# Attention, soft mixture and gated layer on one core: the gated layer issued step by step in an order from a list scheduler

## The chip, the cores and the metric

The kernel runs on one core of a Trainium2 chip. Its time is the device time of one execution in microseconds (us); the kernel before took 598.79 us, the median of three runs (597.3 to 600.0). A core has five engines that each work through an instruction queue of their own in order: TensorE (PE in the profile, its weight loads PEld), VectorE (DVE), ScalarE (ACT), GpSimd (POOL) and SyncE (SP), which here issues every DMA. They wait for each other through semaphores. Matrix products land in PSUM, the accumulator memory, which has eight banks; all else lives in SBUF.

## The reference

Three layers follow each other. Inputs are drawn in float32 (the gated layer's weights come to the kernel as 64-bit words).

```python
# 1: causal attention, 4 batches x 12 heads, 448 positions, head size 64
attn = softmax(mask(q @ k.T / 8)); x = attn @ v          # -> x: 1792 tokens x 768
# 2: soft mixture of 8 experts with 4 slots each
logits = x @ phi                                         # 1792 x 32
slot_input = softmax(logits, over tokens).T @ x          # 32 x 768
slot_out[e] = relu(slot_input[e] @ w1[e]) @ w2[e]        # w1 768x1024, w2 1024x768
x = softmax(logits, over slots) @ slot_out               # 1792 x 768, of rank 32
# 3: gated layer, 1536 hidden columns
out = (sigmoid(x @ w_gate) * (x @ w_val)) @ w_out        # 1792 x 768
```

Since x of layer 3 is (coefficients 1792x32) @ (slots 32x768), the kernel first forms slots @ w_gate and slots @ w_val (32 rows), and then multiplies by the coefficients.

## The kernel before

The attention and the mixture (the first 346 us of the trace) are not touched by the change. What follows is the gated layer.

The 1536 hidden columns are cut into six units u of 256 columns. A unit needs three weight pieces of 1.5 MB, named o, v and g (of w_out, w_val and w_gate), which SP loads in that order, two units ahead where a buffer is free: five buffers `w`. Each piece arrives as 64-bit floats and is turned into 32-bit floats in place by two ACT instructions (L193, L143) and two DVE instructions (L197, L199) over 1536 columns. Then:

- o: ACT finds the largest absolute value (L666), a matmul with ones spreads it over the partitions (`amx`, L138), DVE makes a power of two of it, and the piece is split into two float16 halves `wh` (L145 or L143) and `wl` (L674).
- v and g: twelve matmuls with the slots (`psg`, L685), a maximum on DVE (L688), a copy on ACT (`gh`, L689), a fold matmul (L693), and two float16 halves `st` (L702 on ACT, L704 on DVE).

The main work of a unit has two kinds of steps. A gate step takes one batch of 448 tokens and 128 hidden columns: two matmuls (`psg` L822 and `psv` L823), a sigmoid on ACT (`sg`, L828), the product on DVE (`hs`, L829), a float16 high part (`hhi`, L830, on ACT, DVE or POOL) and a low part on POOL (`hlo`, L831). There are eight gate steps in a unit. An output step takes one tile of 128 tokens: twelve matmuls of 384 columns (L849; 24 of half the rows where a tile lies across two batches, two tiles of 14) into two PSUM banks, `o0` and `o1`, two buffers each. Each half is then evicted and added to the accumulator `oacc` in SBUF: either DVE alone (L861), or ACT into `ev` (L143) and then POOL adds (L859). The first unit only writes `oacc`, without adding. After the last unit a tile is stored.

The order: the loops of the source say for each tile how many preparation steps of the next unit go beside it (`PPI`), and gate steps are issued `LA` = 4 tiles ahead; the framework's own scheduler then moves instructions by its estimates of time, so that the order on an engine is not that of the source. Only the weight loads are pinned to the order of the source (`PINW`). `HIE`, `EV`, `MWE` and `WHE` say by unit which engine makes `hhi`, the two evictions, the maximum and `wh`. The units' weight conversions are done early: by the time the first unit's tiles are out, the pieces of units 1 and 2 and part of unit 3's are converted.

`hid[b, u]` holds `hhi` and `hlo` of a batch and unit, in `NH` = 4 buffers.

Of the kernel before, what the change touches and what calls it, by code (L numbers as in the profile page):

```python
# [1 line left out]

# [5 lines left out]
F32 = mybir.dt.float32  # L8
# [11 lines left out]
def kernel(  # L20
# [44 lines left out]
    PARTS = ((0,), (1,), (2,), (3,), (4,), (5,))  # L65
# [7 lines left out]
    PPI = (1, 3, 3, 6, 4)  # L73
    LAG = 1
    LA = 4
    NH = 4
# [12 lines left out]
    PINW = True  # L89
    PB = (3, 3, 2)  # L90
    HIE = 'PPVAAAVAAAVV'
    EV = 'AAPVVPVVVPVV'
    MWE = 'AAAAAA'
    WHE = 'VVAAAV'
# [27 lines left out]

    def pow2(pool, mx, n, nm):
# [3 lines left out]
        nc.vector.tensor_scalar(p, mx, 2.0 ** -20, None, ALU.max)  # L127
        nc.vector.tensor_scalar(p.bitcast(I32), p.bitcast(I32), 0x7F800000, None, ALU.bitwise_and)
        nc.vector.reciprocal(s, p)
        nc.vector.tensor_scalar(s, s, P14, None, ALU.mult)  # L130
        return p, s

    def spread_sum(pool, ps_pool, tag, am):

        am16 = pool.tile([128, 1], BF16, tag="am16", name="am16")
        nc.vector.tensor_copy(am16, am)
        out_ = ps_pool.tile([128, 1], F32, tag=tag, name="amx")
        nc.tensor.matmul(out_, lhsT=ones, rhs=am16, start=True, stop=True)  # L138
        return out_

    def mult(on, out, in_, x):
        if on == "A":
            nc.scalar.activation(out=out, in_=in_, func=AF.Copy, scale=x)  # L143
        else:
            nc.vector.tensor_scalar(out, in_, x, None, ALU.mult)  # L145

# [18 lines left out]
    for u in range(len(PARTS[0]), FF // UC):  # L165
        worder += w_unit(u)

    wt = {}
    ring = [wpC] * NC + [wpA] * NA
    solo = []  # L170

    def load_w(n=1):
        for _ in range(n):
# [6 lines left out]
            x = nc.sync.dma_start(out=t.bitcast(I32) if key[0] in "ovg" else t, in_=src)  # L180
            if PINW:
                tc.keep_in_program_order(x)
            wt[key] = t

    def from_f64(key):

        t = wt[key].bitcast(I32).rearrange("p a (b w) -> p a b w", w=2)
        lo, hi = t[:, :, :, 0], t[:, :, :, 1]  # L190
        top = wt[key].bitcast(U16).rearrange("p a (b w) -> p a b w", w=4)[:, :, :, 1]

        nc.scalar.activation(out=lo, in_=top, func=AF.Copy, scale=2.0 ** -13, bias=2.0 ** -15 - 0.5)  # L193
        yield
        mult("A", hi.bitcast(F32), hi.bitcast(F32), 2.0 ** -112)
        yield
        nc.vector.scalar_tensor_tensor(lo, hi, -2 ** 31, lo, ALU.bitwise_and, ALU.bitwise_or)  # L197
        yield
        nc.vector.scalar_tensor_tensor(hi, hi, 3, lo, ALU.logical_shift_left, ALU.bitwise_or)  # L199
        yield  # L200
        return hi.bitcast(F32)


    with ExitStack() as actx:
# [28 lines left out]

        class Pinned:

            def __init__(self, engine):
                self.engine = engine

            def __getattr__(self, name):
                f = getattr(self.engine, name)  # L240

                def call(*a, **kw):
                    x = f(*a, **kw)  # L243
                    tc.keep_in_program_order(x)
                    return x
                return call
# [398 lines left out]
    gs_p = ctx.enter_context(rp("gs", 1))  # L645
    wo_p = {}
    st_p = {u: st0 for u in PARTS[0]}
# [6 lines left out]
    unit = [{} for _ in range(FF // UC)]  # L654
# [4 lines left out]
    def prep_o(u, wo):  # L659

        d = unit[u]
        mw = sm1("mw")
        wh = wo_p[u].tile([128, 2, DM], F16, tag=f"wh{(u - 1) % 4}", name="wh")
        wl = wo_p[u].tile([128, 2, DM], F16, tag=f"wl{(u - 1) % 4}", name="wl")
        if MWE[u] == "A":
            nc.scalar.activation(out=wl, in_=wo, func=AF.Abs, accum_out=mw)  # L666
        else:
            nc.vector.tensor_reduce(mw, wo, axis=AX.XY, op=ALU.max, apply_absolute_value=True)
        yield
        am = spread_sum(sm2, ps1, "a", mw)  # L670
        d["pw"], sw = pow2(sm2, am, 1, f"w{u}")
        mult(WHE[u], wh, wo, sw)
        yield
        nc.vector.scalar_tensor_tensor(wl, wo, sw, wh, ALU.mult, ALU.subtract)  # L674
        d["w"] = (wh, wl)
        yield

    def prep_gv(u, nm, w):

        d = unit[u]  # L680
        tg = "a" if nm == "g" else "b"
        ps = ps1.tile([128, UC], F32, tag=tg, name="psg")
        for kc in range(KC):
            g = kc % 4
            nc.tensor.matmul(ps[32 * g:32 * g + 32, :], lhsT=soT[:, kc], rhs=w[:, kc], start=kc < 4, stop=kc + 4 >= KC)  # L685
        gh = gs_p.tile([128, UC], F32, tag="gh", name="gh")
        mv = sm1("m" + nm)
        nc.vector.tensor_reduce(mv, ps, axis=AX.X, op=ALU.max, apply_absolute_value=True)  # L688
        nc.scalar.copy(gh, ps)  # L689
        yield  # L690
        ps = ps1.tile([128, UC], F32, tag=tg, name="psg2")
        mx = spread_sum(sm2, ps1, tg, mv)
        nc.tensor.matmul(ps, lhsT=fold4.rearrange("p a s -> p (a s)"), rhs=gh, start=True, stop=True)  # L693
        p, sc = pow2(sm2, mx, 1, f"{nm}{u}")
        if nm == "g":
            d["ag"] = sm1(f"ag{u}")
            nc.vector.tensor_scalar(d["ag"], p, 2.0 ** -28, None, ALU.mult)
        else:
            d["pv"] = p
        yield  # L700
        st = d[nm] = st_p[u].tile([128, UC], F16, tag=f"{nm}{(u - 1) % 4}", name="st")
        nc.scalar.activation(out=st, in_=ps, func=AF.Copy, scale=sc)  # L702
        yield
        nc.vector.scalar_tensor_tensor(st[64:], ps[64:], sc[64:], st[64:], ALU.mult, ALU.subtract)  # L704
        yield

    def prep(us):

        post = iter(())
        got = {}  # L710

        def conv(key):
# [225 lines left out]
```

## Time and profile before

| | us |
|---|---|
| median of 3 runs | 598.79 |
| the profiled execution | 598.05 |
| its span, first to last instruction | 596.2 |
| first output matmul of the gated layer | 355.13 |
| last output matmul starts | 591.62 |
| TensorE busy, share of the span | 508.3, 85% |
| VectorE / ScalarE / GpSimd busy | 389.8 / 326.6 / 248.6 |
| mean granted clock of TensorE | 0.956 |

The clock is given as a share of full speed: 1.00 is 2.4 GHz and 0.50 is 1.2 GHz, the two levels that occur. A matmul's duration includes its way through the array, and matmuls overlap: what one costs on a busy PE is the distance between the starts of two that follow each other. Instructions of DVE and ACT overlap by some tenths of a microsecond in the same way. A wait is idle time of an engine just before an instruction, put down to the instruction whose semaphore came last.

### The profile page before, as it was taken

The numbers are of one execution on the slowest core, as the hardware profiler recorded it, in microseconds if no ns is written. First come the engines' busy times: TensorE is split into PE (matmuls) and PEld (weight loads), VectorE is DVE, ScalarE is ACT, GpSimd is POOL, SyncE is SP. The second block draws the span as 40 slices with busy tenths as digits, with TensorE's granted clock in tenths as the row PEclk, the third lists the DMA queues.
The fourth block names the chain that finished last, engine by engine and source line by source line (L and its number), as shares of the span: only waits on it lengthen the run. The fifth ranks groups of instructions, "written<-read, shape, count | busy, mean of one in ns | idle before, by whom it ended". The sixth has DMA issues, their size and how long they took to land.

```text
span 596.2 us, 12985 instructions
## 1 busy us (share of the span) xinstructions
PE 508.3 (85%) x4977; PEld 308.1 (52%) x4977; DVE 389.8 (65%) x962; ACT 326.6 (55%) x734; POOL 248.6 (42%) x341
## 2 busy tenths in 40 slices
PE   2899989998999799799924678769989889899997
PEld 1576766675667576455412234434544435455554
DVE  2788877796877887321035038987975957774674
ACT  2677867676777667101152059997857753434400
POOL 6665663655466410000000028406775861445720
PEclk9899999999999999879978689998999989899999
DMA  7756547554674213879999991805305303000044
GB/s 161 199 116 183 159 144 200 160 136 125 182 199 127 80 28 108 317 291 382 404 399 404 407 396 70 300 18 197 121 1 212 107 1 107 0 1 1 2 186 185
DMA packets 95565, 101.59 MB, mean 170 GB/s; under 512 B 68624, under 2 KB 68624, under 8 KB 95504
## 3 DMA queue, kind: packets, MB, share of 16 engines
q1 hardware_dynamic: 95504, 100.77, 51.1%
q8 instruction: 39, 0.64, 0.5%
q14 instruction: 22, 0.18, 0.1%
HBM read 95.26 MB, written 5.51 MB: 169 GB/s over the span
## 4 chain that ended last, share of the span: by engine, by line
PE 60%; ACT 13%; DMA 10%; DVE 6%; issue 4%; POOL 4%; ACTq 0%; DVEq 0%; POOLq 0%; SPq 0%
PE pso L849 20%; PE psP L243 9%; PE psS L243 8%; ACT P L243 4%; DMA w<-in_moe_w_val_dram 4%; PE psX L243 4%; DMA w<-in_moe_w_dram 4%; PE psT L243 4%; PE psh L741 3%; PE so L754 3%; ACT hi L243 3%; DMA w<-in_moe_w_gate_dram 2%; PE psg L685 2%; ACT w L143 2%; DVE hs L829 1%
## 5 line engine op out<-in xcount | busy, mean ns | idle before, releaser
L849 PE MATMUL pso<-wh,hhi 128*128 128x384 f16 (+1 forms) x384 | 109.3, 336 | 4.9 <-ACT oacc L143 4.8
L849 PE MATMUL pso<-wh,hlo 128*128 128x384 f16 (+1 forms) x384 | 107.1, 330 | 6.6 <-POOL hlo L831 6.6
L849 PE MATMUL pso<-wl,hhi 128*128 128x384 f16 (+1 forms) x384 | 107.8, 331 | 0.0
L243 ACT ACTIVATE P<-psS,nm 128x256 f32<-128x256 f32 (+3 forms) x168 | 81.9, 504 | 31.5 <-PE psP L243 16.7
L849 PEld LDWEIGHTS <-hhi 128*128 128x128 f16 (+1 forms) x768 | 65.3, 102 | 62.0 <-issue 24.8
L243 DVE CUSTOM_DVE_ANT_0 psS<-psS,cmaskq,sc 128x256 f32<-128x256 f32 (+1 forms) x144 | 66.6, 489 | 31.2 <-PE psS L243 28.7
L831 POOL TENSOR_TENSOR hlo<-hs,hhi 128x448 f16<-128x448 f32 x48 | 59.4, 1246 | 58.1 <-PE amx L138 22.5
L861 DVE SCALAR_TENSOR_TENSOR oacc<-pso,osc,oacc 128x384 f32<-128x384 f32 x98 | 58.5, 612 | 32.6 <-PE pso L849 32.0
L243 PE MATMUL psP<-ident,P 128*128 128x128 f32 x384 | 59.1, 286 | 17.6 <-ACT P L243 11.6
L859 POOL TENSOR_TENSOR oacc<-oacc,ev 128x384 f32<-128x384 f32 x42 | 53.2, 1277 | 30.2 <-ACT ev L143 29.8
L243 PEld LDWEIGHTS psP<-ident,P 128*128 128x128 f32 x384 | 40.9, 142 | 35.6 <-ACT P L243 21.2
L243 POOL TENSOR_TENSOR sq<-sq 128x512 bf16<-128x512 bf16 (+1 forms) x88 | 56.2, 638 | 6.5
L830 POOL CAST hhi<-hs 128x448 f16<-128x448 f32 x8 | 11.9, 1495 | 104.6 <-DVE hs L829 104.6
L849 PEld LDWEIGHTS <-hlo 128*128 128x128 f16 (+1 forms) x384 | 34.4, 101 | 32.0 <-POOL hlo L831 8.7
L243 PE MATMUL psV<-PT,v 128*64 128x64 f32 (+3 forms) x672 | 48.0, 293 | 0.3 <-ACT PT L243 0.3
L197 DVE SCALAR_TENSOR_TENSOR w<-w 128x1536 int32<-128x1536 int32 x18 | 33.8, 1879 | 16.4 <-ACT w L143 16.4
L243 PEld LDWEIGHTS psV<-PT,v 128*64 128x64 f32 x672 | 32.0, 137 | 20.9 <-issue 14.0
L193 ACT ACTIVATE w<-w 128x1536 int32<-128x1536 uint16 x18 | 30.1, 1674 | 17.6 <-DMA w<-in_moe_w_gate_dram 7.7
L143 ACT ACTIVATE ev<-pso,osc 128x384 f32<-128x384 f32 x42 | 23.4, 582 | 27.5 <-PE pso L849 24.4
L829 DVE SCALAR_TENSOR_TENSOR hs<-psv,sg 128x448 f32<-128x448 f32 x48 | 29.0, 618 | 13.2 <-ACT sg L828 8.3
L243 POOL TENSOR_SCALAR r<-sum 128x7 f32<-128x7 f32 x24 | 5.8, 242 | 76.1 <-ACT P L243 69.0
L828 ACT ACTIVATE sg<-psg,ag 128x448 f32<-128x448 f32 x48 | 29.5, 637 | 14.7 <-PE psg L822 11.8
(278 smaller groups left out, 980.3 us busy)
## 6 DMA issues: line engine op xcount, KB each, us to landing
w<-in_moe_w_dram SPq DMA_DIRECT2D x32, 1536.0 KB, 9.5
w<-in_moe_w_out_dram SPq DMA_DIRECT2D x6, 1536.0 KB, 12.7
w<-in_moe_w_val_dram SPq DMA_DIRECT2D x6, 1536.0 KB, 12.8
w<-in_moe_w_gate_dram SPq DMA_DIRECT2D x6, 1536.0 KB, 6.7
out_dram<-oacc SPq DMA_DIRECT2D x14, 384.0 KB, 2.3
q<-in_q_dram SPq DMA_DIRECT2D x36, 128.0 KB, 3.0
k<-in_k_dram SPq DMA_DIRECT2D x36, 128.0 KB, 3.0
v<-in_v_dram SPq DMA_DIRECT2D x36, 128.0 KB, 7.9
```

What stands on the lines that cost most here:

```text
L143: nc.scalar.activation(out=out, in_=in_, func=AF.Copy, scale=x)
L193: nc.scalar.activation(out=lo, in_=top, func=AF.Copy, scale=2.0 ** -13, bias=2.0 ** -15 - 0.5)
L197: nc.vector.scalar_tensor_tensor(lo, hi, -2 ** 31, lo, ALU.bitwise_and, ALU.bitwise_or)
L243: x = f(*a, **kw)
L741: nc.tensor.matmul(ps[32 * g:32 * g + 32, :], lhsT=slotT[:, kc, :], rhs=w[:, kc % 3, 256 * g:256 * g + 256], start=kc == 0, stop=kc == KC - 1)
L754: nc.tensor.matmul(so[32 * c:32 * c + 32, :], lhsT=hT[:, i, 32 * g:32 * g + 32], rhs=w[:, f % 4, 256 * c:256 * c + 256], start=e == 0 and ...
L828: nc.scalar.activation(out=sg, in_=pg, func=AF.Sigmoid, scale=d["ag"])
L829: nc.vector.scalar_tensor_tensor(hs, pv, 1.0 / P14, sg, ALU.mult, ALU.mult)
L831: nc.gpsimd.tensor_tensor(lo[:, c], hs, hi[:, c], ALU.subtract)
L849: nc.tensor.matmul(ps[n][o:o + m], lhsT=hid[b, u][x][:, c, s0:s0 + m], rhs=y[:, c, 384 * n:384 * n + 384], start=f, stop=l)
L859: nc.gpsimd.tensor_tensor(a, a, x, ALU.add)
L861: nc.vector.scalar_tensor_tensor(a, ps[n], osc, a, ALU.mult, ALU.add)
```

## The change

The gated layer is no longer written as loops. Each piece of work (a load, a conversion, a gate matmul pair, a sigmoid, an output step of twelve matmuls, an eviction and so on) becomes one step, 700 in all, with the engines it may run on and a length for each, its predecessors, the buffers that it takes and holds, and a due time. A loop then issues one step after another: of those that can start soonest in its own bookkeeping (within `WAIT` = 0.3 us on the same engine) the one with the earliest due time; where a step may run on ACT or DVE, on the one that would end first. Every instruction so issued is kept in that order on its engine. The lengths, and the due times made of them, are numbers of the source. Besides:

- `hhi` is made on ACT or DVE, no longer on POOL; in the order that comes out there are 24 on each.
- In units 1 to 4 half 0 of every tile is evicted by ACT and added by POOL (56 adds; before there were 42, in units 1, 2 and 4), half 1 by DVE. In unit 5 DVE takes both halves. In unit 0 the first-time evictions are 14 on ACT and 14 on DVE (before 28 on ACT).
- A unit's pieces are converted during the unit before it. The counts by stretch between the first evictions of two units are, for DVE's 1536-column conversions, 8, 6, 7, 6, 3 and 0 (and three pieces ahead of that, as before, for unit 0).
- The sigmoid's table is loaded on ACT after expert 5, by a small instruction on `warm`, and not at the first sigmoid.
- `NH` is 8, the copies `gh` have two buffers, g is prepared before v in unit 0, and the last tile is stored in two halves of 384 columns.

The weight loads go out in the same order, but some into other buffers. Before, the g pieces of units 3, 4 and 5 take the buffer of the o piece of the unit before, which is free after that unit's `wl`; now those of units 3 and 4 take the buffer of its v piece, free after v's products. Unit 2's took v's before as well, and unit 5's still takes o's.

Core of the diff:

```diff
-    NH = 4
+    NH = 8
+    LAND = (8.2, 12.0, 16.0)
+    LDT = 3.9
+    SLACK, MARGIN, WAIT = 1.6, 0.6, 0.3
-    HIE = 'PPVAAAVAAAVV'
-    EV = 'AAPVVPVVVPVV'
...
+            nc.scalar.activation(out=warm, in_=hT[:, 0, :1], func=AF.Sigmoid)
...
+            for f, e, c in ((a1, "A", 1.68), (a2, "A", 1.65), (d1, "V", 1.9), (d2, "V", 1.9)):
+                op((f,) + k, lambda f=f, k=k: f(k), {e: c}, [was], use=w)
...
+                op((hhi,) + k, call(hhi), {"A": 0.57, "V": 0.53}, [(hsv,) + k], new=[] if c else [("hid", ("hid", b, u))],
+                   use=[("hs",) + k], pick=True)
+                op((hlo,) + k, call(hlo), {"G": 1.25}, [(hhi,) + k], use=[("hs",) + k])
...
+            op((outp,) + k, lambda k=k: outp(*k), {"P": c}, [(hlo, b, u, c_) for b in bs for c_ in range(2)] + ([(wlo, u)] if u else []),
+               new=[("o0", ("o0",) + k), ("o1", ("o1",) + k)], use=[("hid", b, u) for b in bs], behind=chained("out", (outp,) + k),
+               due=now)
+            for n in range(2):
+                e = {"A": 0.62, "V": 0.5} if u == 0 else {"A": 0.6} if n == 0 and u < NU - 1 else {"V": 0.61}
...
+    while todo:
+        got = [(y[1], ops[j].due, j, y) for j in sorted(todo) for y in [soonest(j)] if y]
+        m = min(got)
+        _, _, j, y = min((x for x in got if x[3][2] == m[3][2] and x[0] <= m[0] + WAIT), key=lambda x: (x[1], x[0]))
+        x = ops[j]
+        x.end, _, x.e = y
+        free[x.e] = x.end
+        for r, z in x.new:
+            held[r].append(z)
+        x.f(*([x.e] if x.pick else []))
+        todo.remove(j)
```

On GpSimd, from the first gate step of unit 0, the kernel before has (names: `hhi`, `hlo` the halves of a gate step, `oacc<-oacc,ev` an add):

```order
L830 CAST hhi<-hs 128x448 x2
L831 TENSOR_TENSOR hlo<-hs,hhi 128x448 x2
L830 CAST hhi<-hs 128x448
L831 TENSOR_TENSOR hlo<-hs,hhi 128x448
L830 CAST hhi<-hs 128x448 x2
L831 TENSOR_TENSOR hlo<-hs,hhi 128x448 x2
```

and now, from the same place:

```order
L128 TENSOR_TENSOR hlo<-hs,hhi 128x448 x12
L128 TENSOR_TENSOR oacc<-oacc,ev 128x384 x4
L128 TENSOR_TENSOR hlo<-hs,hhi 128x448 x2
L128 TENSOR_TENSOR oacc<-oacc,ev 128x384 x3
L128 TENSOR_TENSOR hlo<-hs,hhi 128x448 x2
L128 TENSOR_TENSOR oacc<-oacc,ev 128x384 x4
L128 TENSOR_TENSOR hlo<-hs,hhi 128x448 x2
```

The casts are gone from it, and adds and low parts alternate through units 1 to 4, 14 adds and 8 low parts in each.

On ScalarE, at the first gate steps of unit 0, before (`w<-w` a conversion, `oacc<-pso` an eviction of unit 0, `wl,mw` the maximum of an o piece):

```order
L828 ACT_TABLE_LOAD
L828 ACTIVATE sg<-psg_5109,ag_5068 128x448
L828 ACTIVATE sg<-psg_5113,ag_5068 128x448
L828 ACTIVATE sg<-psg_5132,ag_5068 128x448
L193 ACTIVATE w<-w 128x1536
L143 ACTIVATE w<-w 128x1536
L828 ACTIVATE sg<-psg_5136,ag_5068 128x448
L193 ACTIVATE w<-w 128x1536
L143 ACTIVATE w<-w 128x1536
L828 ACTIVATE sg<-psg_5204,ag_5068 128x448
L143 ACTIVATE oacc<-pso,osc_5073 128x384 x4
```

and now:

```order
L128 ACTIVATE sg<-psg,ag_5060 128x448 x2
L128 CAST hhi<-hs 128x448
L128 ACTIVATE sg<-psg,ag_5060 128x448 x2
L128 ACTIVATE w<-w 128x1536
L128 ACTIVATE sg<-psg,ag_5060 128x448
L128 ACTIVATE w<-w 128x1536 x3
L128 ACTIVATE oacc<-pso,osc_5073 128x384
L128 ACTIVATE w<-w 128x1536 x2
L128 ACTIVATE sg<-psg,ag_5060 128x448 x2
```

The table load has left this place, a high part has come in, and evictions stand singly between conversions. (All instructions that the new order issues carry one line, L128, that of the helper which pins them.)

## Rows read from the trace of the kernel before

**Rows 1.** Windows by unit's evictions: us, then busy (count) of PE, PEld, DVE, ACT, POOL; clock.
```profile
361.00:409.00 48.00, 38.05 (x239) 20.10 (x238) 41.83 (x55) 45.72 (x64) 23.67 (x16) 0.96 0.27 101
409.00:448.00 39.00, 36.11 (x241) 19.32 (x239) 30.61 (x51) 27.02 (x39) 28.66 (x23) 1.00 0.34 122
448.00:492.00 44.00, 39.45 (x252) 19.20 (x254) 31.23 (x54) 29.27 (x42) 29.89 (x23) 0.96 0.30 108
492.00:533.00 41.00, 37.96 (x245) 19.83 (x246) 32.93 (x68) 15.13 (x25) 13.28 (x11) 0.96 0.11 39
533.00:566.00 33.00, 33.00 (x223) 19.50 (x221) 17.84 (x42) 14.64 (x27) 19.85 (x20) 1.00 0.01 1
566.00:593.00 27.00, 25.94 (x181) 15.08 (x178) 18.76 (x32) 1.16 (x2) 4.10 (x4) 1.00 0.49 190
```
**Rows 2.** Waits of PE, 361 to 593: total us, times, longest.
```profile
PE pso L849 <- POOL hlo L831: 6.6, 4, 2.1
...
PE pso L849 <- ACT oacc L143: 4.8, 5, 1.6
```
**Rows 3.** Windows of the same columns at the lower clock, the first and last.
```profile
403.80:407.20 3.40, 3.40 (x12) 1.53 (x11) 3.03 (x6) 3.28 (x5) 2.75 (x4) 0.50 0.00 0
...
509.60:513.00 3.40, 3.14 (x10) 1.31 (x9) 2.68 (x7) 2.02 (x4) 2.09 (x3) 0.50 0.00 0
```
**Rows 4.** PE in order of time: start, us, instruction; first and last output matmul.
```profile
355.13 0.84 PE L849 MATMUL pso<-wh,hhi 128*128 128x384 f16 x2
...
591.62 0.33 PE L849 MATMUL pso<-wh,hlo 128*128 128x384 f16 x1
```
**Rows 5.** PE in order of time: where steps of each kind start.
```profile
372.21 0.66 PE L685 MATMUL psg<-w,soT 128*32 128x256 f32 x8
372.81 0.34 PE L849 MATMUL pso<-wh,hhi 128*128 128x384 f16 x1
...
383.96 0.68 PE L693 MATMUL psg<-gh,fold 128*128 128x256 f32 x2
...
557.86 0.35 PE L822 MATMUL psg<-cT,st 128*128 128x448 f16 x1
...
558.24 0.35 PE L822 MATMUL psg<-cT,st 128*128 128x448 f16 x1
...
583.85 0.35 PE L849 MATMUL pso<-wh,hhi 128*64 128x384 f16 x2
...
585.92 0.34 PE L849 MATMUL pso<-wh,hhi 128*128 128x384 f16 x1
...
587.88 0.33 PE L849 MATMUL pso<-wh,hhi 128*128 128x384 f16 x1
```
**Rows 6.** ACT in order of time: the table load.
```profile
351.18 1.28 ACT L828 ACT_TABLE_LOAD   x1
```
**Rows 7.** DVE, then POOL, in order of time, side by side.
```profile
429.05 2.38 DVE L199 SCALAR_TENSOR_TENSOR w<-w 128x1536 int32<-128x1536 int32 x1
431.48 2.43 DVE L197 SCALAR_TENSOR_TENSOR w<-w 128x1536 int32<-128x1536 int32 x1
...
429.93 2.36 POOL L859 TENSOR_TENSOR oacc<-oacc,ev 128x384 f32<-128x384 f32 x1
432.25 2.54 POOL L831 TENSOR_TENSOR hlo<-hs,hhi 128x448 f16<-128x448 f32 x1
```
**Rows 8.** By line: ns shortest/median/longest, first and last start.
```profile
L859 POOL TENSOR_TENSOR oacc<-oacc,ev x42: 986/998/2630, 409.7 to 564.4; 128x384 f32<-128x384 f32 x42
...
L831 POOL TENSOR_TENSOR hlo<-hs,hhi x48: 1025/1036/2604, 354.9 to 571.3; 128x448 f16<-128x448 f32 x48
...
L830 DVE CAST hhi<-hs x16: 382/390/1111, 402.8 to 570.2; 128x448 f16<-128x448 f32 x16
...
L197 DVE SCALAR_TENSOR_TENSOR w<-w x18: 1748/1760/2531, 306.7 to 502.5; 128x1536 int32<-128x1536 int32 x18
```
**Rows 9.** Waits of ACT, 361 to 593, for a weight load.
```profile
ACT w L193 <- DMA w<-in_moe_w_gate_dram: 7.7, 4, 3.5
```

More of the change, by code (lines that the diff above doesn't have):

```diff
@@ L653, with osc @@
     soT = cT_p.tile([128, KC, NS], F32, name="soT")
-    unit = [{} for _ in range(FF // UC)]
+    unit = [{} for _ in range(NU)]
     def sm1(nm, n=1):
         return sm2.tile([128, n], F32, tag=nm, name=nm)
-    def prep_o(u, wo):
+    def osc(u):
         d = unit[u]
[L662 to L676, printed above, removed]
@@ new lines, in gv, with sig @@
+    def gv(b, u, c):
+        cols = slice(128 * c, 128 * c + 128)
+        for nm, tg in (("g", "a"), ("v", "b")):
+            ps = buf[nm, b, u, c] = ps1.tile([128, S], F32, tag=tg, name="ps" + nm)
+            on.te.matmul(ps, lhsT=unit[u][nm][:, cols], rhs=cT[:, b * S:(b + 1) * S], start=True, stop=True)
+    def sig(b, u, c):
+        sg = buf["sg", b, u, c] = hs_p.tile([128, S], F32, tag="sg", name="sg")
+        on.ac.activation(out=sg, in_=buf.pop(("g", b, u, c)), func=AF.Sigmoid, scale=unit[u]["ag"])
@@ new lines, in spans, with outp @@
+    def spans(i):
+        out_ = []
+        o = 0
+        while o < 128:
+            b, s0 = divmod(128 * i + o, S)
+            n = min(128 - o, S - s0)
+            out_.append((o, n, b, s0))
+            o += n
+        return out_
+    def outp(u, i):
+        ps = [pso.tile([128, 384], F32, tag=f"o{n}", name="pso") for n in range(2)]
+        for n in range(2):
+            buf["o", u, i, n] = ps[n]
+        wh, wl = unit[u]["w"]
+        for c in range(2):
+            for x, y in ((0, wh), (0, wl), (1, wh)):
+                for n in range(2):
+                    for o, m, b, s0 in spans(i):
+                        on.te.matmul(ps[n][o:o + m], lhsT=hid[b, u][x][:, c, s0:s0 + m], rhs=y[:, c, 384 * n:384 * n + 384],
+                                     start=c == 0 and x == 0 and y is wh, stop=c == 1 and x == 1)
@@ new lines @@
+    for x in reversed(ops):
+        c = min(x.on.values())
+        for d in x.deps:
+            ops[d].due = min(ops[d].due, x.due - c * SLACK - MARGIN)
+        for d in x.behind:
+            ops[d].due = min(ops[d].due, x.due - 0.001)
+    room = dict(w=NC + ND, a=2, b=2, o0=2, o1=2, hid=NH, ev=2, sg=2, hs=2, gs=2)
+    held = {r: [] for r in room}
+    free = dict.fromkeys("PAVGD", 0.0)
+    on.te, on.ve, on.ac, on.po, on.sp = (Pinned(x) for x in (nc.tensor, nc.vector, nc.scalar, nc.gpsimd, nc.sync))
@@ new lines, with soonest @@
+    todo = set(range(len(ops)))
+    def soonest(j):
+        x = ops[j]
+        if not all(hasattr(ops[d], "end") for d in x.deps + x.behind):
+            return None
+        t = x.first
+        for r, _ in x.new:
+            if len(held[r]) >= room[r]:
+                for k in tiles[held[r][-room[r]]]:
+                    if not hasattr(ops[k], "end"):
+                        return None
+                    t = max(t, ops[k].end + 0.11)
+        best = None
+        for e, c in x.on.items():
+            s = max([t, free[e]] + [ops[d].end + (0.11 if ops[d].e != e else 0.0) for d in x.deps])
+            if best is None or s + c < best[0]:
+                best = (s + c, s, e)
+        return best
```

398 lines of the change are left out of this document (200 added, 198 removed).

## The prediction

> **What bounds the kernel now.** I read the windows of the gated layer first, then PE's waits, then the clock, then the engines side by side. The windows, cut at the first eviction of each unit, show two things [rows 1]. The stretches of units 0 to 5 take 48, 39, 44, 41, 33 and 27 us although each issues the same 14 output steps. And another engine is nearly full only in the first: ACT 45.7 of 48. In 409 to 533 the fullest beside PE is DVE with 31 to 33 of 39 to 44. PE is busy throughout only in 533 to 566.
>
> How much of that is work? Distances between starts give PE's prices [rows 5]: a whole tile 587.88 - 585.92 = 1.96 us, a tile across two batches 585.92 - 583.85 = 2.07, a gate pair 558.24 - 557.86 = 0.38. Eight of the 24 records of the v and g products take 372.81 - 372.21 = 0.60, so a unit's take 1.8; two folds of at most 0.68 and three tiny spreads I put at 1.6 together, an estimate. A unit's output is 12 x 1.96 + 2 x 2.07 = 27.7, its gates 8 x 0.38 = 3.0, the preparation of the next 3.4. From the first output matmul on there remain 6 x 27.7 + 43 x 0.38 + 5 x 3.4 = 199.5 us. The stretch from 355.13 to 591.95 [rows 4] takes 236.8. So 37 us there are not work at full clock. The waits name a part of it: for POOL's `hlo` 6.6 and for ACT's evictions 4.8 [rows 2]. Three windows of 3.4 us at 0.50 cost 1.7 each, about 5 [rows 3]; PE had waited before each. The rest are gaps too small to be named. Those 37 us are the most that an order can give back. The first 346 us keep their instructions and order.
>
> **The change part by part.** *Lead-in.* The table load of 1.28 us at 351.18 [rows 6] moves to a place in the mixture where ACT is waiting for weights anyway; if it weren't, it would cost at most its 1.28. Here it hid in part behind DVE's last `st`, and PE has five gate pairs ahead of its first output matmul, the third of which waits for a sigmoid. I let that matmul start at 354.5 and not 355.13, with 353.8 (the whole load gained) and 355.5 as ends.
>
> *Unit 0.* ACT is full there because 28 evictions and the conversions of two and a half units stand in it. Half of the evictions go to DVE and the conversions are spread over five units, so ACT falls well below PE's 27.7 + 7 x 0.38 + 3.4 = 33.8. What is late next is DVE, which takes 14 evictions, eight conversions and the casts that POOL had, and then PE itself. I take 35.5: PE's work and a third of the 4.8 us that PE waited for ACT evictions [rows 2].
>
> *Units 1 to 4.* PE's work is 27.7 + 3.0 + 3.4 = 34.1 in each. The second bound is one that no single engine shows. At 429 DVE converts while POOL adds [rows 7]: the add starts at 429.93 and ends at 432.29, about 1.0 after the first conversion's end (431.43); the second conversion starts at 431.48 and takes 2.43 instead of 1.76; the `hlo` behind it, ready at 432.25, takes 2.54 instead of 1.04. Each runs at its undisturbed length after the other has ended, and the lengths by line have the same two values, 1.00 and 2.63 for the add, 1.04 and 2.60 for `hlo`, 1.76 and 2.53 for a conversion, 0.39 and 1.11 for DVE's cast [rows 8]. So I add up the undisturbed lengths of these as if they shared one door. In a unit now: 6 conversions and one `wl` (same size, same price) 7 x 1.76 = 12.3, four casts 4 x 0.39 = 1.6, 14 adds 14.0, 8 `hlo` 8.3: together 36.2, more than PE's 34.1. Unit 2 has seven conversions, 38.0; unit 4 three of them and `wh`, 32.7. In the Trainium skill, "SBUF — State Buffer", section "Who interferes with whom", DVE with two SBUF inputs or in a two-port mode and GpSimd lock each other out for a whole instruction; the trace agrees in these rows.
>
> How full can that door be? In 409 to 448 it held 6 x 1.76 + 3 x 0.39 + 23 POOL instructions at 1.02 = 35.2 of 39 us, 90%, and that order did not aim at it. At 90% units 1 to 4 would take 40.2, 42.2, 40.2 and 36.3; if contention were all hidden, 34.1 each. There is no row between, since the source's lengths (1.9 for a conversion, 1.25 and 1.29 on POOL) hold the average of past contention but no lock. I take the middle: 37.2, 38.2, 37.2 and 35.2.
>
> *Weights.* ACT waited 7.7 us in four waits for g pieces [rows 9]. The g loads of units 3 and 4 now start when v's products free a buffer, several tiles ahead of the `wl` that they waited for; unit 5's still follows a `wl`. That leaves one wait of 1.9, of which PE's two output buffers cover about a tile. If the others stayed it would be 4 x 1.9 on ACT, which has that slack. Both lie inside the middle taken.
>
> *Eight buffers.* Nothing: gate steps of the next unit's first two batches are issued after tile 10, when tiles 3 and 6 have long freed the four old slots. Without the cover they would cost a wait for a tile, at most 2 us a unit; PE shows no such wait now.
>
> *Unit 5 and the end.* PE's work is 27.7 + 4 x 0.38 = 29.2, DVE has only evictions and four products: 29.5. The end was 596.2 - 591.95 = 4.25 after the last matmul; half a tile less in the last store gives 0.4 of it, an estimate.
>
> *Sum.* 35.5 + 37.2 + 38.2 + 37.2 + 35.2 + 29.5 = 212.8. 354.5 + 212.8 = 567.3, and 3.85 to the end makes a span of 571.1. The profiled execution has 598.05 - 596.2 = 1.85 outside its span: **573 us**. It is 0.7 below the median of the runs shown, which I leave alone.
>
> **The rivals.** *PE alone bounds.* The door's contention falls into slack of DVE and POOL. For it: 533 to 566 is full of PE work with 20 POOL instructions. Against it: DVE has no conversion there, and the sum over units 0 to 4 of the door (about 31 + 36.2 + 38.0 + 36.2 + 32.7 = 174) is as long as PE's (170). Time: 354.5 + 199.5 + 3.85 + 1.85 = **560**.
>
> *The door stays at 90%.* Locks upset a fixed order, since an instruction that is held holds all behind it. For it: DVE and POOL ran at that share in the only comparable stretch. Time: 37 + 40.2 + 42.2 + 40.2 + 36.3 + 30 = 225.9, which ends at **586**.
>
> *Slower: evictions behind conversions.* On ACT, half 0 of every tile in units 1 to 4 now stands in one fixed row with conversions of 1.65 us and cannot pass them. PE may run two tiles ahead, then waits. In unit 0 of before it waited 4.8 us over 14 tiles for such evictions [rows 2], 0.34 a tile; over 70 tiles that would be 24 on 560, still faster. The mechanism decides from 42 / 70 = 0.6 us a tile, and at 0.7 the time is 560 + 49 = **609**. Against it: with the same evictions and conversions ACT was busy 27 of 39 us in unit 1 of before [rows 1], and conversions stand singly between evictions.
>
> *The order does not come out.* An engine could be given another row than the planned one; but the instructions are pinned, and the rows of POOL and ACT show the plan. I give it no chance of its own.
>
> **How the numbers follow.** Forecast (566 to 580) 0.55; PE alone 0.20; door at 90% (580 to 592) 0.18; evictions behind conversions, no faster than now, 0.07, of which 0.04 slower. A measurement of this kernel tells about 0.5% from no change, 3 us. So faster 0.93, same 0.03, slower 0.04. The range for 8 in 10 runs from the first rival to the second, 560 to 587.
>
> **What would show it.** Right: output matmuls from 354 to about 567; unit 0's stretch falls from 48 to about 36 with ACT no longer full; units 1 to 3 take 36 to 39 with POOL busy over 28 us each, adds and conversions often at 2.4 us, and PE waiting for `hlo` and evictions by a few tenths at a time; fewer than three windows at 0.50. Wrong: stretches of 34 to 35 with those long instructions present (the door is shared but hidden), stretches over 40 (the fixed order passes the locks on to PE), ACT waiting for g pieces in each unit, or PE waiting over 0.5 us a tile for ACT's evictions.

## The result, and the profile after

The changed kernel takes 570.02 us (median of 4 runs, 568.24 to 572.36) where the kernel before takes 598.58 beside it: 0.953 of it, 95% interval 0.948 to 0.957. Timed again beside later runs it came to 569.69 (6 runs), 0.952 (0.949 to 0.956). The profiled execution took 569.02, with a span of 567.1. The forecast was 573, in a range of 560 to 587.

The windows by unit's evictions, cut as in [rows 1] (same columns), now read:

```profile
358.60:393.30 34.70, 33.77 (x239) 19.21 (x237) 32.47 (x57) 29.56 (x40) 11.73 (x8) 1.00 0.40 141
393.30:428.00 34.70, 34.43 (x241) 19.82 (x240) 33.43 (x55) 27.32 (x39) 31.20 (x22) 1.00 0.29 98
428.00:465.70 37.70, 34.51 (x241) 19.88 (x240) 33.88 (x56) 27.44 (x41) 32.25 (x23) 1.00 0.35 127
465.70:500.00 34.30, 34.28 (x241) 19.45 (x239) 31.22 (x55) 26.25 (x39) 32.48 (x24) 1.00 0.29 105
500.00:535.40 35.40, 34.33 (x240) 19.41 (x239) 31.34 (x53) 20.42 (x34) 29.12 (x23) 1.00 0.05 20
535.40:563.90 28.50, 27.54 (x190) 15.99 (x187) 18.67 (x34) 3.98 (x7) 6.13 (x6) 1.00 0.46 180
```

The second column is the stretch, the third PE's busy time in it. Units 0 to 5 took 48, 39, 44, 41, 33 and 27 us before. Unit 0 has given 13; units 1 to 3 have given 4 to 7 each; unit 4 has taken 2.4, since work on unit 5's weights, which before was done by then, now stands in it; unit 5 has taken 1.5, since more of its own matmuls fall behind its border (190 of PE's records for 181). Another 4 lie ahead of the first eviction, which came 6 us after the first output matmul and now comes 2 after it. PE is the fullest engine of every stretch, and the granted clock is 1.00 in all, where [rows 3] had stretches at 0.50. PE's waits in the gated layer, to hold against [rows 2] (total us, times, longest):

```profile
PE pso L128 <- ACT ev L128: 3.3, 3, 2.4
PE psv L128 <- DVE hs L128: 1.1, 1, 1.1
PE psg L128 <- ACT gh L128: 0.9, 1, 0.9
PE pso L128 <- DVE oacc L128: 0.8, 1, 0.8
```

The waits for `hlo` (6.6) are gone, and so are 5.2 us for sigmoids, the second largest wait of the kernel before:

```profile
PE psg L822 <- ACT sg L828: 5.2, 8, 2.3
```

Those for ACT's evictions went from 4.8 to 3.3, of which 2.4 is a single one. From the first output matmul to the last, to hold against [rows 4]:

```profile
356.31 0.35 PE L128 MATMUL psv<-cT,st 128*128 128x448 f16 x1 [1.14 <-DVE hs L128]
356.50 0.49 PE L128 MATMUL pso<-wh,hhi 128*128 128x384 f16 x2
...
562.45 0.49 PE L128 MATMUL pso<-wh,hlo 128*128 128x384 f16 x2
```

That is 562.94 - 356.50 = 206.4 us for 236.8 before, against 199.5 of work by the prediction's prices. Between the two profiled executions the gain is 598.05 - 569.02 = 29.0: this 30.4, less the 1.4 by which the first output matmul is later. The contention of [rows 7] and [rows 8] has not gone: by shape, mean ns of one behind the busy time,

```profile
L128 POOL TENSOR_TENSOR hlo<-hs,hhi 128x448 f16<-128x448 f32 x47 | 77.0, 1651 | 36.3 <-ACT hhi L128 29.5 <-DVE hhi L128 6.4 <-DVE am L128 0.4
L128 POOL TENSOR_TENSOR oacc<-oacc,ev 128x384 f32<-128x384 f32 x56 | 69.8, 1264 | 13.5 <-ACT ev L128 13.5
...
L128 DVE SCALAR_TENSOR_TENSOR w<-w 128x1536 int32<-128x1536 int32 x30 | 60.4, 2015 | 0.0
```

beside undisturbed lengths of 1.04, 1.00 and 1.76 us. PE hardly waits for it, but in unit 2. There DVE has three conversions with single evictions between them, GpSimd two low parts and an add, and ACT's third eviction has no buffer until that add has ended (DVE, POOL, ACT and PE, in this order):

```profile
428.67 1.99 DVE L128 SCALAR_TENSOR_TENSOR w<-w 128x1536 int32<-128x1536 int32 x1
430.58 0.60 DVE L128 SCALAR_TENSOR_TENSOR oacc<-pso,osc,oacc 128x384 f32<-128x384 f32 x1
431.11 2.07 DVE L128 SCALAR_TENSOR_TENSOR w<-w 128x1536 int32<-128x1536 int32 x1
...
433.63 2.06 DVE L128 SCALAR_TENSOR_TENSOR w<-w 128x1536 int32<-128x1536 int32 x1
...
429.00 5.08 POOL L128 TENSOR_TENSOR hlo<-hs,hhi 128x448 f16<-128x448 f32 x2
434.04 4.42 POOL L128 TENSOR_TENSOR oacc<-oacc,ev 128x384 f32<-128x384 f32 x3
...
436.57 0.58 ACT L128 ACTIVATE ev<-pso,osc 128x384 f32<-128x384 f32 x1 [4.37 <-POOL oacc L128]
...
437.20 0.48 PE L128 MATMUL pso<-wh,hhi 128*128 128x384 f16 x2 [2.38 <-ACT ev L128]
```

### The profile page after: what moved, and what is told of

The parts are those of the page before. It is cut to its first block, busy times and chain, and to the rows that moved or that the text cites. A ratio compares the mean times of both kernels' runs of the same rounds, so it can differ in the third digit from the quotient of the medians.

```text
span 567.1 us, 12997 instructions
## 1 busy us (share of the span) xinstructions
PE 495.1 (87%) x4977; PEld 309.3 (55%) x4977; DVE 398.1 (70%) x970; ACT 326.8 (58%) x735; POOL 271.6 (48%) x347
## 4 chain that ended last, share of the span: by engine, by line
PE 65%; ACT 10%; DMA 7%; DVE 6%; POOL 5%; issue 3%; SPq 1%; DVEq 0%; ACTq 0%; POOLq 0%
PE pso L128 23%; PE psP L128 9%; PE psS L128 8%; DMA w<-in_moe_w_dram 7%; ACT P L128 4%; PE psX L128 4%; PE psT L128 4%; PE psg L128 4%; PE so L738 3%; PE psh L725 3%; ACT hi L128 3%; POOL hlo L128 3%; SPq L128 1%; POOL oacc L128 1%; PE psL L128 1%
## 5 line engine op out<-in xcount | busy, mean ns | idle before, releaser
L128 POOL TENSOR_TENSOR hlo<-hs,hhi 128x448 f16<-128x448 f32 x48 | 78.2, 1643 | 132.1 <-ACT hhi L128 125.3
L128 ACT ACTIVATE P<-psS,nm 128x256 f32<-128x256 f32 (+3 forms) x168 | 82.0, 504 | 31.1 <-PE psP L128 16.3
L128 PEld LDWEIGHTS <-hhi 128*128 128x128 f16 (+1 forms) x768 | 65.3, 101 | 54.0 <-issue 14.7
L128 DVE CUSTOM_DVE_ANT_0 psS<-psS,cmaskq,sc 128x256 f32<-128x256 f32 (+1 forms) x144 | 66.6, 489 | 33.3 <-PE psS L128 30.8
L128 PE MATMUL pso<-wh,hhi 128*128 128x384 f16 (+1 forms) x384 | 83.2, 328 | 4.2 <-ACT ev L128 3.3
L128 PE MATMUL pso<-wh,hlo 128*128 128x384 f16 (+1 forms) x384 | 82.3, 326 | 0.0
L128 PE MATMUL pso<-wl,hhi 128*128 128x384 f16 (+1 forms) x384 | 82.2, 326 | 0.0
L128 POOL TENSOR_TENSOR oacc<-oacc,ev 128x384 f32<-128x384 f32 x56 | 69.8, 1264 | 13.5 <-ACT ev L128 13.5
L128 PE MATMUL psP<-ident,P 128*128 128x128 f32 x384 | 59.5, 287 | 17.7 <-ACT P L128 11.7
L128 PEld LDWEIGHTS psP<-ident,P 128*128 128x128 f32 x384 | 41.2, 142 | 35.9 <-ACT P L128 21.5
L128 DVE SCALAR_TENSOR_TENSOR w<-w 128x1536 int32<-128x1536 int32 x30 | 60.4, 2015 | 0.0
L128 POOL TENSOR_TENSOR sq<-sq 128x512 bf16<-128x512 bf16 (+1 forms) x88 | 56.2, 639 | 6.5
L128 DVE SCALAR_TENSOR_TENSOR oacc<-pso,osc,oacc 128x384 f32<-128x384 f32 x84 | 49.8, 610 | 13.2 <-PE pso L128 12.6
L128 ACT ACTIVATE w<-w 128x1536 int32<-128x1536 uint16 (+1 forms) x30 | 49.3, 1656 | 1.9 <-DMA w<-in_moe_w_gate_dram 1.9
L128 ACT ACTIVATE ev<-pso,osc 128x384 f32<-128x384 f32 x56 | 32.5, 585 | 29.7 <-PE pso L128 15.9
L128 PE MATMUL psV<-PT,v 128*64 128x64 f32 (+3 forms) x672 | 48.0, 293 | 0.3 <-ACT PT L128 0.3
L128 PEld LDWEIGHTS <-hlo 128*128 128x128 f16 (+1 forms) x384 | 33.8, 101 | 20.8
L128 POOL TENSOR_SCALAR r<-sum 128x7 f32<-128x7 f32 x24 | 5.8, 243 | 78.9 <-ACT P L128 71.7
L128 PEld LDWEIGHTS psV<-PT,v 128*64 128x64 f32 x672 | 32.0, 137 | 20.9 <-issue 14.0
L128 ACT ACTIVATE hi<-psT,qks 128x448 f16<-128x448 f32 x48 | 27.8, 630 | 15.7 <-PE psT L128 15.7
L725 PE MATMUL psh<-w,slotT 128*32 128x256 f32 x384 | 28.7, 427 | 8.3 <-DMA w<-in_moe_w_dram 7.8
```

The costliest lines, as they stand in the source:

```text
L725: nc.tensor.matmul(ps[32 * g:32 * g + 32, :], lhsT=slotT[:, kc, :], rhs=w[:, kc % 3, 256 * g:256 * g + 256], start=kc == 0, stop=kc == KC - 1)
```

## The experiments

The theory was: the gain is the order that stands on the engines, above all conversions that are spread and preparation that comes before PE needs it; the division among engines, the buffers and the pin as such are worth little; the door of DVE and GpSimd is mostly hidden. Rivals: the division among engines; the pin, whatever order it keeps; the buffers; the door as the bound of units 1 to 4.

**The pin taken away** (`unpinned`):

```diff
-    on.te, on.ve, on.ac, on.po, on.sp = (Pinned(x) for x in (nc.tensor, nc.vector, nc.scalar, nc.gpsimd, nc.sync))
```

> The changed kernel with the same steps, engines, buffers and source order, but without the pin: the framework's own scheduler may move the gated layer's instructions by its estimates again, as it does in the kernel before. Theory (the gain is the order that stands on the engines): much of it goes, since that scheduler pulls conversions and gate steps together again; 580 to 600, with units' stretches of 38 to 45 and windows at the lower clock back. Rival (the gain is the division among engines and the buffers, any order does): 568 to 575.

591.04 us, 0.987 (0.984 to 0.990): 21 of the 28.6 us are lost with the same steps, engines and buffers. Its units take 55.3, 33.2, 40.8, 32.6, 38.5 and 26.2, so nearly all of the loss stands in unit 0 (20.6; the rest add up to 171.3 for 170.6). The forecast of windows at 0.50 held there; units of 38 to 45 came only twice. What DVE does on weight pieces in unit 0 tells why (stretch, busy time and count of its instructions on `w`, clock; the kernel before, the changed kernel and this one):

```profile
361.00:409.00 48.00, 32.77 (x18) 0.96 0.27 101
...
358.60:393.30 34.70, 16.00 (x9) 1.00 0.40 141
...
356.80:412.10 55.30, 30.75 (x17) 0.88 0.29 107
```

The framework's scheduler pulls the conversions of later units forward again. DVE does unit 1's factors and `st` between them, and when unit 0's last tile has been evicted, at 392.7, PE has nothing to do until these are there:

```profile
398.45 0.93 PE L794 MATMUL psv<-cT,st 128*128 128x448 f16 x2 [7.53 <-DVE st L714]
```

From the first to the last output matmul it takes 230.8 us, so that 24.4 of the 30.4 gained there are lost. One thing the pin doesn't explain: units 1 to 5, which took 184 in the kernel before, are as short without it as with it. What shortens them is among the things that both share, the order in which the steps are issued, the division among engines and the buffers, and no run separates all of these; the runs below show that the division alone doesn't do it (`engines`) and that eight value buffers aren't needed for it (`nh4`).

**The pin alone** (`pinned_before`: the kernel before, its loops' order kept):

```diff
+    nc = SimpleNamespace(tensor=Pinned(nc.tensor), vector=Pinned(nc.vector), scalar=Pinned(nc.scalar),
+                         gpsimd=Pinned(nc.gpsimd), sync=nc.sync)
```

> The kernel before with its gated layer kept on every engine in the order in which its loops issue it, so that the framework's scheduler moves nothing; the division among engines and the buffers are those of before. Theory (what matters is which order is kept): the loops' order puts conversions of whole pieces in a row between tiles, so evictions wait behind them: 595 to 625, no gain from the pin as such. Rival (the framework's moves are what costs the kernel before its 37 us): 570 to 582.

659.17 us, 1.103 (1.100 to 1.106), slower than either theory said. Conversions are spread here as well (8, 7, 9, 6 and 8 instructions of DVE on pieces in units 0 to 4), and it doesn't help, because a one-column matmul of the preparation stands in PE's row before its input is there (PE's waits):

```profile
PE amx L244 <- DVE am L244: 46.8, 15, 8.7
PE psg L244 <- DVE w L244: 11.7, 6, 3.5
```

So it is neither the pin nor the spreading by itself: a kept order gains only where the next instruction on each engine is one whose input is ready.

**The division among engines alone** (`engines`, on the kernel before):

```diff
-    HIE = 'PPVAAAVAAAVV'
-    EV = 'AAPVVPVVVPVV'
+    HIE = 'AV' * 6
+    EV = 'AV' + 'PV' * 4 + 'VV'
...
-    WHE = 'VVAAAV'
+    WHE = 'VAAAVV'
```

> The kernel before with only the changed kernel's division among engines: high parts on ACT and DVE by turns and none on GpSimd, half 0 of units 1 to 4 on ACT and GpSimd and half 1 on DVE, unit 0's first evictions half ACT, half DVE, unit 5 on DVE alone; loops, order and four buffers as before. Theory (order): unit 0's stretch gains, as ACT loses 14 evictions, but conversions still stand bunched and the door is as full as in the changed kernel: 585 to 598. Rival (division among engines): 570 to 578.

603.69 us, 1.009 (1.006 to 1.011): 0.9% slower, so outside both expectations. Unit 0 took 51.3 though half of its evictions had left ACT, whose busy time there fell only from 45.7 to 41.0, and units 1 to 4 took 160 for 157.

**Unit 0's evictions all on ACT** (`u0_act`, on the changed kernel):

```diff
-                e = {"A": 0.62, "V": 0.5} if u == 0 else ...
+                e = {"A": 0.62} if u == 0 else ...
```

> The changed kernel with all 28 first-time evictions of unit 0 on ACT, as before, instead of 14 on ACT and 14 on DVE; the list scheduler plans around it. Theory (unit 0 gains because conversions are spread, 8 of DVE's in it for 18 before; the division of its evictions is secondary): ACT gets 14 x 0.6 = 8.4 us more on 30, about 38.5, so unit 0 takes 37 to 40 for 34.8, and the whole 572 to 576. Rival (unit 0 gains because half of its evictions left ACT): its stretch goes back to 45 or more, and the whole to 580 or more.

574.64 us, 0.962 (0.960 to 0.963). The time is the theory's, the place is not: unit 0 still takes 34.8 us, since the list scheduler puts less of ACT's other work in it (10 instructions on pieces for 12). Unit 3 pays, where a wait of PE for `ev` of 2.5 us has appeared, like the one that unit 2 has, and both units hold a stretch at 0.50:

```profile
358.40:393.20 34.80, 32.91 (x232) 18.89 (x230) 26.82 (x45) 31.21 (x50) 12.43 (x8) 1.00 0.45 159
...
428.60:466.80 38.20, 35.81 (x242) 20.14 (x240) 32.78 (x57) 26.79 (x38) 29.55 (x23) 0.96 0.34 125
466.80:507.10 40.30, 37.82 (x251) 21.07 (x250) 34.88 (x56) 27.27 (x40) 34.85 (x24) 0.96 0.28 103
```

The 13 us of unit 0 thus don't hang on the split of its evictions; `unpinned` has that split and takes 55.3, so they are the order's. The halves on DVE, with the order that is planned for them, are worth about 5 us in all, and elsewhere.

**Four value buffers** (`nh4`):

```diff
-    NH = 8
+    NH = 4
```

> The changed kernel with four value buffers instead of eight (the instructions on every engine keep the same rows). Theory (the gain is the order): the second set of buffers costs and gives nothing, since the gate steps of the next unit come after tile 10, when the old slots are long free: 570, within 1.5 us of the changed kernel. Rival (the buffers let the gate steps run ahead): a wait of PE's output matmuls or of DVE's high parts for old slots at each of five unit borders, 1 to 2 us each, so 575 to 580.

567.43 us, 0.950 (0.946 to 0.954), the changed kernel's time within the scatter; 206.6 us from the first to the last output matmul. Eight buffers give nothing.

**The adds left out** (`no_adds`):

```diff
-        on.po.tensor_tensor(a, a, buf.pop(("e", u, i, n)), ALU.add)
+        buf.pop(("e", u, i, n))
```

> The changed kernel without GpSimd's 56 adds of units 1 to 4; half 0 of these units is evicted and not summed, so part of the result is left out. What stays is the order, every conversion, and 48 low parts on GpSimd. Theory (units 1, 3 and 4 already run at PE's own work, and the shared door costs only in unit 2, through ACT's evictions that wait for adds): unit 2 falls from 37.7 to 34.5 and little else changes, so 3 us less than the changed kernel, 565 to 568 by its median of 570. Rival (the door bounds units 1 to 4 as forecast, and they would be shorter without it): every one of the four stretches falls by 2 us or more, 8 to 12 us in all, 558 to 562.

565.0 us (562.5 to 567.4), 0.943 (0.940 to 0.947), 5 less than the changed kernel. Units 1 to 4 take 33.4, 35.8, 35.2 and 35.0, together 139.4 for 142.1: all 56 adds cost 2.7 us there, most of it in unit 2 (which fell less than to the expected 34.5), and from the first to the last output matmul 2.0 (204.4 for 206.4). This trace has a stretch at 0.50 at its first output matmuls that the changed kernel's lacks, with 3.6 us to the first eviction for 2.1, so the adds cost some 3.5, an estimate from these two. That is far from the 8 to 12 of the rival: the adds didn't hold units 1 to 4 as forecast.

**Four eviction buffers**, with the order kept (`ev4_same`) and with the list scheduler told of them (`ev4`):

```diff
-    NH = 8
+    NH = 4
...
+    ev_p = ctx.enter_context(rp("evp", 4, side="right"))
...
-            x = buf["e", u, i, n] = hs_p.tile([128, 384], F32, tag="ev", name="ev")
+            x = buf["e", u, i, n] = ev_p.tile([128, 384], F32, tag="ev", name="ev")
```

In `ev4_same` the list scheduler goes on counting eight value and two eviction buffers, which keeps the order; in `ev4` it counts four of each.

> The changed kernel with four buffers for ACT's evictions instead of two (and four value buffers to make room); the order is kept as with two. In unit 2 of the changed kernel ACT's eviction waits 4.4 us for GpSimd's add to free one of two buffers, and PE then waits 2.4 us for ACT. Theory (the door is passed on to PE through these two buffers): that wait goes and with it 2 to 3.3 us, 566 to 568 beside 569 to 570. Rival (GpSimd is late there whatever ACT does, and the wait comes back at the next low part): no change, within 1 us.

> Four eviction buffers as in the run with the kept order, but the list scheduler is told of four, so that the order changes with them. Theory (only the coupling of ACT and GpSimd in unit 2 is to be had, 2 us): the same as with the kept order, 564 to 567. Rival (the planned order leans on two buffers to keep GpSimd close behind ACT; with four it lets adds pile up, and low parts come late behind them): PE waits for low parts at unit borders, 568 to 574.

565.42 us (0.945, 0.943 to 0.947) and 564.87 (0.945, 0.944 to 0.947). These beat both the kernel before and the changed one. Unit 2 falls to 35.9, and PE's waits for `ev` from 3.3 to 0.3 (the kept order):

```profile
426.50:462.40 35.90, 34.83 (x241) 19.77 (x240) 34.58 (x57) 27.80 (x40) 32.75 (x23) 1.00 0.38 133
```

So GpSimd's lateness reached PE through ACT's two buffers. Both runs have four value buffers as well, so `nh4`, whose instructions stand in the same order as those of `ev4_same`, is the run to hold that one against: 567.43 and 565.42 by the medians, 206.6 and 204.6 from the first to the last output matmul. The buffers are thus worth 2.0 us. The 4 to 5 to the changed kernel's medians are more, and the next run shows where at least part of the rest can be.

**The changed kernel again** (`after_again`, no edit):

> The changed kernel itself, timed again beside the runs below on the same chip, so that differences of 2 to 5 us can be told. Theory: 567 to 571; its span from the first to the last output matmul 206 to 207 us again (206.4 in its first trace), while the time of that first matmul may differ by some us, as between the traces so far, where no instruction ahead of it differs.

569.69 us (566.3 to 572.9). In this execution the stretch took 209.0 and not 206.4, missing its expectation by 2, with the same instructions. Two stretches have the lower clock, one at the first output matmuls and one at the wait in unit 2, which here ends at 440.00; the same places are at 1.00 in the first trace:

```profile
357.60:361.00 3.40, 3.40 (x13) 1.62 (x12) 2.26 (x4) 3.40 (x4) 2.22 (x3) 0.54 1.01 395
439.20:442.60 3.40, 2.60 (x9) 1.24 (x9) 2.03 (x4) 3.23 (x5) 3.06 (x4) 0.59 0.02 5
...
356.50:359.90 3.40, 3.40 (x22) 2.06 (x21) 3.37 (x7) 3.40 (x4) 2.19 (x3) 1.00 1.01 396
437.20:440.60 3.40, 3.40 (x26) 1.66 (x26) 2.82 (x6) 3.40 (x6) 2.26 (x3) 1.00 0.02 5
```

Beside the same waits of PE, of 1.1 and 2.4 us, one execution has these stretches and the other has not; the two go with the 2.6 us between 209.0 and 206.4. Neither trace of the four-buffer kernels has such a stretch in the gated layer; that this makes their times lie closer (564.4 to 565.4 for the second) is likely, but not shown by single traces.

**The table load put back** (`table_late`):

```diff
-            nc.scalar.activation(out=warm, in_=hT[:, 0, :1], func=AF.Sigmoid)
```

> The changed kernel with the sigmoid's table loaded at the first sigmoid, as in the kernel before. Theory (the load there lies beside DVE's last weight half and PE's first gate pairs, and the second sigmoid's queue has slack): between 0 and 0.7 us more than the changed kernel. Rival (the load stands on the path to the first output matmul): its whole 1.3 us more.

574.27 us, 0.958 (0.956 to 0.961), over 4 us more than the changed kernel and so more than either side said. On the path to the first output matmul the rival was right. From the transposes of the slots (`psst`) to the first output matmul it takes 358.43 - 347.39 = 11.04 us, where the traces with the early load and the same row on PE up to there have 9.5 to 9.8; the third gate pair now waits for the first sigmoid:

```profile
354.94 0.35 PE L128 MATMUL psg<-cT,st 128*128 128x448 f16 x1 [1.17 <-ACT sg L128]
...
358.10 0.53 PE L128 MATMUL psv<-cT,st 128*128 128x448 f16 x1 [1.02 <-DVE hs L128]
358.43 0.84 PE L128 MATMUL pso<-wh,hhi 128*128 128x384 f16 x2
```

What more there is in this trace goes with two stretches at 0.50 in the gated layer; from the first to the last output matmul it takes 210.2 for 206.4. That the load's place brings these about isn't shown, since the changed kernel has such stretches in one execution and not in another.

**The door by itself** (`door`, a block ahead of the changed gated layer):

```diff
+    for _ in range(6):
+        conv()
...
+    for k in range(8):
+        add(k)
...
+    for k in range(12):
+        conv()
+        add(k)
+        add(k + 1)
```

> The changed kernel with a block of its own ahead of the gated steps, on memory that is overwritten later: six DVE instructions of a conversion's form and size alone, then eight GpSimd adds of 384 columns alone, then twelve of the former on DVE beside 24 adds on GpSimd, with nothing else between. It is read from the trace, not from the time, which is longer by the block. If the two engines exclude each other for whole instructions of the undisturbed lengths (1.76 and 1.00, as the prediction added them up), the side-by-side part takes 12 x 1.76 + 24 x 1.00 = 45 us. If the lock covers less than an instruction's length, as a cycle of 2.5 us for a conversion and an add in unit 2 of the changed kernel says (0.26 less than the sum), it takes 12 x 2.5 + 12 x 1.00 = 42 or less. If they don't exclude each other, 24 us.

Six conversions alone, eight adds alone, then both side by side:

```profile
362.18 10.72 DVE L128 SCALAR_TENSOR_TENSOR oacc<-oacc 128x1536 int32<-128x1536 int32 x6
...
373.37 7.63 POOL L128 TENSOR_TENSOR oacc<-oacc 128x384 f32<-128x384 f32 x8
...
381.23 3.55 DVE L128 SCALAR_TENSOR_TENSOR oacc<-oacc 128x1536 int32<-128x1536 int32 x2
...
384.81 24.63 DVE L128 SCALAR_TENSOR_TENSOR oacc<-oacc 128x1536 int32<-128x1536 int32 x10
409.48 0.62 DVE L128 SCALAR_TENSOR_TENSOR hs<-psv,sg 128x448 f32<-128x448 f32 x1
...
383.11 40.31 POOL L128 TENSOR_TENSOR oacc<-oacc 128x384 f32<-128x384 f32 x24
```

From start to start a conversion alone costs 10.72 / 6 = 1.79 us and an add 7.63 / 8 = 0.95. Side by side the block takes 383.11 + 40.31 - 381.23 = 42.2 us, as the second of the three expectations has it. The first two conversions still start 1.79 apart; the ten behind them, with one add beside each, come every (409.48 - 384.81) / 10 = 2.47 us, close to the 2.5 expected from unit 2. That is 0.27 less than 1.79 + 0.95 = 2.74, and 0.29 less than the 1.76 + 1.00 that the prediction added up. The engines exclude each other, but for somewhat less than what the records call an instruction's length.

**The door told to the list scheduler** (`door_known`):

```diff
+    def door(x, e):
+        return e == "G" or e == "V" and x.on["V"] in (1.76, 0.39)
...
+        if door(x, x.e):
+            free["X"] = x.end
```

> The changed kernel with the shared door put into the list scheduler: DVE's conversions, low weight halves and casts and everything on GpSimd may not overlap in its bookkeeping, at undisturbed lengths (1.76, 0.39, 1.04 and 1.00 us); the order follows from that (four value buffers). Theory (PE's last waits come from contention that the planned order does not know): unit 2's 3 us go, 565 to 568. Rival (in the run the two engines take less than the sum of these lengths, as units 1 and 3 show, so the plan puts preparation too late): PE waits for low parts or for wh at unit borders, 570 to 580.

577.56 us, 0.966 (0.963 to 0.969): the rival's side. Units 0 and 4 take 40.3 and 39.6, and PE's waits are for preparation and not for low parts:

```profile
PE amx L128 <- DVE am L128: 4.2, 3, 2.0
PE psg L128 <- DVE hs L128: 4.2, 3, 2.0
```

Preparation comes late in this plan. The lengths were changed together with the lock, so which of the two does it stays open.

## Why the prediction was right, point by point

The time came 3 us below the forecast, but not by the forecast's own account of units 1 to 4: in units 1 and 3 one of its signs of being wrong came, stretches of 34 to 35 with the long instructions present. That the total is so near is in part luck, since a lead-in that was 2.0 too short stands against a gated layer that was 6.4 too long.

- *What bounds.* Right: 37 us of the stretch were not work, and 30 of them have come back. That it takes the kept order is shown now for unit 0 and for the whole: without the pin 21 of the 28.6 are lost, the division among engines alone loses 6, four value buffers change nothing. What shortens units 1 to 5, which stay short without the pin, is open.
- *Lead-in.* Wrong by 2.0 (356.50 for 354.5). Of that 1.4 arose ahead of the gated layer: `psst` starts at 346.77 for 345.38 before, and at 344.01 in the run with four value buffers, where no instruction ahead of it differs. The step that failed is the gain of 0.6: from `psst` it takes 9.73 us for 9.75. The early load [rows 6], now here, hidden before a wait for weights,

```profile
300.33 1.28 ACT L759 ACT_TABLE_LOAD   x1
```

  is worth 1.3 to 1.5 and not 0.6, as `table_late` shows; but PE's row now has the fifth gate pair whole ahead of the first output matmul, where before its `psv` came later, and that `psv` waits 1.14 us for DVE's product. The gain was priced too low and the loss not at all. The first output matmul was a poor mark, too: before, PE began the tile and then waited 0.99 us for a sigmoid that stood behind conversions in ACT's row, and the first evictions stood behind two more (ACT, then PE, of the kernel before):

```profile
355.86 1.58 ACT L143 ACTIVATE w<-w 128x1536 f32<-128x1536 f32 x1
357.35 0.61 ACT L828 ACTIVATE sg<-psg,ag 128x448 f32<-128x448 f32 x1
...
361.46 1.05 ACT L143 ACTIVATE oacc<-pso,osc 128x384 f32<-128x384 f32 x2
...
358.01 0.35 PE L822 MATMUL psg<-cT,st 128*128 128x448 f16 x1 [0.99 <-ACT sg L828]
```

  Now the tile runs through. That is the 4 us ahead of the first eviction, which the forecast had inside unit 0.
- *Unit 0.* 34.7 for 35.5. The size was right, its reason only in half: of the two I named, spread conversions and split evictions, the second isn't needed (`u0_act`), and the first isn't enough by itself (`pinned_before` has it and takes 54.0).
- *Units 1 to 4.* 34.7, 37.7, 34.3 and 35.4 for 37.2, 38.2, 37.2 and 35.2. This is the term that was mis-sized. I added durations, as if a door were held for all of each, and wrote that the rows agree with a lock for a whole instruction. To the hundredth, [rows 7] already showed less. The add ends 432.29 - 431.43 = 0.86 after the first conversion, not "about 1.0", and the second conversion ends 431.48 + 2.43 - 432.29 = 1.62 after the add, not 1.76; from conversion to conversion it is 431.48 - 429.05 = 2.43 with an add between, where 1.76 + 1.00 is 2.76. With the block's price, 0.29 less for each conversion or `wl` that meets a GpSimd instruction, a unit's 36.2 becomes 36.2 - 7 x 0.29 = 34.2, level with PE's 34.1, and unit 2's 38.0 becomes 38.0 - 8 x 0.29 = 35.7; both are estimates, since they let each of these meet one. What came is units 1 and 3 near PE's work, and only unit 2, with three conversions close behind each other and two `ev` buffers, passes the lock on, as 37.7; with four buffers it takes 35.9. That the door sets this 35.9 isn't shown: without the adds the unit takes 35.8. The 90% that served as the other end was no limit of the door: by the prediction's lengths units 1 and 3 now hold 36.2 us of it in 34.7 and 34.3. (`wh` in unit 4, priced at 1.76 like a conversion, took 1.08.) In the Trainium skill, "Perfetto Trace Analysis", section "GPSIMD Engine Instruction", the advice is to time GpSimd by the distance between starts and not by the reported duration; the block agrees, 0.95 for the recorded 1.00 of [rows 8]. For PE I had taken distances between starts, and not here. Alone, these distances take only 0.02 off a pair (2.74 for 2.76); the other 0.27 show only where the two engines run side by side.
- *Weights.* Right: one wait of ACT for a g piece is left, of 1.9 [rows 9].

```profile
ACT w L128 <- DMA w<-in_moe_w_gate_dram: 1.9, 1, 1.9
```

- *Eight buffers.* Right: nothing.
- *Unit 5 and the end.* 28.5 for 29.5. The end after the last matmul is 567.1 - 562.94 = 4.2 and not 3.85: half a tile less in the last store gave nothing that shows.
- *Sum.* 573.0 + 2.0 (lead-in) - 6.4 (206.4 for 212.8) + 0.3 (end) + 0.1 (outside the span) = 569.0.
- *The rivals.* PE alone (560) described units 1 and 3 better than the forecast did; it misses by the lead-in and by 206.4 - 199.5 = 6.9, of which unit 2's wait of 2.4 is the largest part that has a name. The door at 90% fell. Evictions behind conversions: 3.3 us in 70 tiles, 0.05 a tile where 0.6 decides; the one long wait was for a buffer that GpSimd held.

## What to carry to other kernels

When engines run in order, the order is a resource of its own: here one list of steps took 570 us in the planned order and 591 in the framework's, and the kernel before 598 in the framework's and 659 in that of its loops. Price two engines that exclude each other from start to start while they run side by side, not by adding recorded lengths; the plan made with the sum was 8 us worse than the one that knew no lock, though its lengths differed as well. Where a late engine reaches the bottleneck through another's buffers, two more buffers can be worth more than planning the order anew: they gave 2 us here, the new order for them 0.6 more, and eight buffers elsewhere nothing.

## What the runs showed of the hardware

- DVE's conversion and GpSimd's add exclude each other for less than the sum of what they take alone: 2.47 us a pair side by side, 1.79 and 0.95 alone. The time lost shows in the records of the one that waits: in [rows 8] the longest add took 2.63 us for a usual 1.00, the longest conversion 2.53 for 1.76.
- Instructions that follow each other on DVE overlap by about 0.1 us, not by "some tenths": in unit 2 the eviction at 430.58 starts 0.08 before the conversion from 428.67 ends.
- The table load costs the path its 1.28 us and little more: the sigmoid behind it starts at 354.25, 1.30 after the load's start at 352.95 (in `table_late`).
- The same program shows 3.4 us stretches at the granted clock of 0.50 in one execution and not in another, the two seen here beside waits of PE of 1 to 2.4 us; the transposes at the start of the gated layer came between 344.01 (`nh4`) and 347.91 us (`after_again`) in executions with the same instructions ahead of them.
